# Three real products instead of four in half of a forward transform, and an edge column computed inside the loop before it

## The chip, the cores and the metric

The kernel runs on one core of a Trainium2 chip. TensorE multiplies matrices into PSUM, VectorE and ScalarE read PSUM and SBUF, GpSimd does small elementwise work in SBUF, and DMA queues that are fed by SyncE, ScalarE and GpSimd move data. The metric is the time of one execution on the device in microseconds, and lower is better. The kernel before takes 1229.07 us (median of 3 runs, 1228.78 to 1231.65).

## The reference

The input x has 2048 rows (s) of 1024 values. Its rows are normalised, and two branches work on the result.

```python
xn = _layernorm(x, axis=-1)
X = rfft2(xn) * (w_r + 1j * w_i)          # branch A: filter in the frequency domain
s = irfft2(X)
h = silu(einsum("bsd,df->bsf", xn, w1))   # branch B: 1024 -> 3584 -> 1024
g = silu(einsum("bsf,fd->bsd", h, w2))
return x + s * g
```

Both branches must come out in single precision. TensorE works on halves, so a factor is split into a high and a low half (float16), and a product is the sum of high x high, high x low and low x high: three passes.

## The kernel before

TensorE's order is one list that Python writes at build time. Its backbone is branch B: 112 blocks of 24 matmuls of 512 columns (`mm1`, tile `pa`, L458), then 56 blocks of 42 such matmuls (`mm2`, tile `pb`, L541 to L543). The 56 blocks are seven products (a fast 2x2 scheme over halves of the matrices) of eight blocks each; `pb2_0` is product 2, block 0. Their left factors `ht` are fetched from HBM on ScalarE's queue two blocks ahead (`load_h`, L517).

Branch A is a background job in five stages, each a Python generator that issues a little work at each `yield`: layer norm, forward transform over the row (`fd_gen`), forward transform over s and filter (`f_gen`), the edge column (`edge_gen`), inverse transforms (`i_gen`). `work()` is called after each block, and inside each `mm2` block after 21 of its 42 matmuls; each call advances the background by up to three steps, and stops earlier when a metered VectorE clock is more than `LEAD` = 1 us ahead of a metered TensorE clock. The meter charges VectorE 0.12 us and 1.05 ns per element of a row for each instruction. So the places of the background's matmuls among the blocks are fixed at build time; at run time each engine goes through its own list, and semaphores make it wait.

The forward transform over s: s is written as 4a + c, and `fd_gen` leaves, for each c and each column block j of 128 frequencies, complex values V split in halves, stored in HBM as `vd[j]`. `f_gen` has 16 units u = 4q + j. A unit takes frequency class q, computes for each c the complex product of a 128x128 matrix (`kq`) with V (`mat`, tile `fx`), combines the four c by a radix-4 step (`xb`, `xd`, `X`), multiplies by the filter (`wq`, `T1`, `T2`, `Y`), makes the first radix-4 step of the inverse (`yb`, `yd`, `Z`; GpSimd does an eighth of it), and splits the result in halves (`zq`; ScalarE writes the high one in `high_z`, L992, VectorE the low one in `low_z`, L997). `mat` is:

```python
for c in range(4):
    o = ps[:, c].rearrange("m r k -> m (r k)")
    for n, (kh, vh) in enumerate(((0, 0), (0, 1), (1, 0))):
        nc.tensor.matmul(o, k[:, c, kh, 1], v[:, c, vh], ...)                              # L965, 256 columns
        nc.tensor.matmul(ps[:, c, 0], k[:, c, kh, 2], v[:, c, vh, 128:256], ...)           # L966, 128
        nc.tensor.matmul(ps[:, c, 1], k[:, c, kh, 0], v[:, c, vh, 0:128], ...)             # L967, 128
```

A unit's result is one tile of two PSUM banks, and the pool `pt` has two of them. ScalarE copies the half c = 2, 3 to SBUF (`xc`, L986), and VectorE adds and subtracts PSUM and copy (L1015, L1016). `mat(u + 1)` is issued inside unit u. `zq` holds four units in one buffer: the first unit of a class (u = 4, 8, 12) can only write it when the four DMAs `zd<-zq` of the class before have landed, and that wait stands in ScalarE's list, in front of whatever ScalarE has to do next.

The edge column (frequency 512 of the row transform, and its partner 0) needs every class, so `edge_gen` ran as a job of its own after unit 15: 12 small copies on GpSimd, nine float32 matmuls of 8 and 24 columns (`eps`, L1096 to L1098; each goes through TensorE in two passes), some 32 GpSimd instructions, and a store and four loads through HBM (`zpd`, `zps`). Then the job `switch` closes the filter's buffers and opens those of the inverse: `zt` is loaded from `zd` (L1173), GpSimd writes the edge column into it (`edge_in`, L1184), and the first inverse matmuls (`iu`, L1215) read it.

## Time and profile before

| what | value |
|---|---|
| time, median of 3 runs | 1229.07 us (1228.78 to 1231.65) |
| time of the profiled execution | 1231.15 us |
| its span, first to last instruction | 1229.4 us |
| TensorE busy | 1218.5 us, 6992 matmuls |
| VectorE busy | 999.7 us, 81% |
| ScalarE busy | 471.5 us, 38% |
| forward transform over s (`fx`) | from 570.7 to 814.5 us |
| `eps` | from 838.0 to 840.8 us |
| first `iu` | at 892.3 us |

A profile's matmul lasts longer than the step to the next one, because matmuls are pipelined. Where several follow each other, the price of one is the distance between two starts. The span leaves out 1.75 us of the profiled execution's time. A row of the timeline reads: start, duration, engine, line, operation, out<-in, shape, count, and in brackets how long the engine had been idle and what it waited for.

### The profile page before, as it was taken

How to read it: one execution, taken by the hardware profiler on the slowest of the kernel's cores; microseconds unless marked ns; L12 is line 12 of the kernel's file. 1: busy time of each engine (PE TensorE's matmuls, PEld its weight loads, DVE VectorE, ACT ScalarE, POOL GpSimd, SP SyncE). 2: the span in 40 equal slices, each digit the busy share in tenths (PEclk: the TensorE clock that was granted, in tenths of full speed). 3: DMA queues.
4: the chain of work that ended last, by engine and by line, in shares of the span. 5: the costliest groups of instructions: out<-in, count | busy, mean ns of one | idle time of the engine just before them, and what ended most of it. 6: DMA issues, size and time to landing. Idle time of an engine off the chain costs nothing.

```text
span 1229.4 us, 19034 instructions
## 1 busy us (share of the span) xinstructions
PE 1218.5 (99%) x6992; PEld 619.8 (50%) x6992; DVE 999.7 (81%) x1974; ACT 471.5 (38%) x614; POOL 119.7 (10%) x247
## 2 busy tenths in 40 slices
PE   8999999999999999999999999999999999999998
PEld 5544445444544454445445555544455545555545
DVE  7778998799899889887969899885186678798885
ACT  6675343343554555435433222122032222233212
POOL 3320000000000000010001121114111111000000
PEclk9999999999999999999999999999999999999999
DMA  8887477645669797759899989987979999998686
GB/s 250 186 199 182 139 235 218 202 131 166 201 188 299 226 296 225 217 188 285 178 301 236 299 249 192 276 243 244 285 195 286 276 291 331 305 355 327 199 268 253
DMA packets 279550, 295.77 MB, mean 241 GB/s; under 512 B 48544, under 2 KB 207264, under 8 KB 279072
## 3 DMA queue, kind: packets, MB, share of 16 engines
q1 hardware_dynamic: 259440, 235.76, 65.6%
q10 hardware_dynamic: 15984, 51.45, 12.2%
q0 software_dynamic: 4032, 7.34, 3.5%
q8 instruction: 55, 0.90, 0.3%
q14 instruction: 39, 0.32, 0.1%
HBM read 185.95 MB, written 102.25 MB: 234 GB/s over the span
## 4 chain that ended last, share of the span: by engine, by line
PE 70%; DVE 11%; DMA 8%; issue 3%; ACT 3%; POOL 0%; SPq 0%; ACTq 0%; DVEq 0%; POOLq 0%
PE pa L458 41%; PE pb L541 8%; PE pb L543 8%; PE pb L542 8%; DVE Z L1066 2%; DMA zd<-zq 2%; PE id L1305 2%; DVE T L1031 1%; ACT xp L740 1%; DMA sd<-s 1%; DVE w L256 1%; PE iu L1215 1%; DMA ht<-hd_sum_d 1%; DMA wq<-in_A_w_i_dram 1%; DVE zq L997 1%
## 5 line engine op out<-in xcount | busy, mean ns | idle before, releaser
L458 PE MATMUL pa<-xnT,w 128*128 128x512 f16 x2688 | 584.1, 379 | 1.2 <-ACT w L253 0.7
L458 PEld LDWEIGHTS <-w 128*128 128x128 f16 x2688 | 261.4, 98 | 313.1 <-issue 1.2
L541 PE MATMUL pb<-w,ht 128*128 128x512 f16 (+2 forms) x812 | 301.2, 373 | 0.0
L543 PE MATMUL pb<-w,ht 128*128 128x512 f16 (+2 forms) x812 | 301.0, 373 | 0.0
L542 PE MATMUL pb<-w,ht 128*128 128x512 f16 (+2 forms) x812 | 301.0, 372 | 0.0
L543 PEld LDWEIGHTS <-ht 128*128 128x128 f16 x812 | 79.6, 98 | 91.5 <-issue 0.8
L542 PEld LDWEIGHTS <-ht 128*128 128x128 f16 x812 | 79.6, 98 | 87.1 <-issue 0.8
L541 PEld LDWEIGHTS <-ht 128*128 128x128 f16 x812 | 79.6, 98 | 87.0 <-issue 0.6
L467 ACT ACTIVATE h<-pa,s 128x512 f32<-128x512 f32 x112 | 75.8, 678 | 117.6 <-PE pa L458 94.1
L253 ACT ACTIVATE w<-jr,sc 128x512 f16<-128x512 f32 x98 | 68.1, 713 | 84.4 <-DMA jr<-in_B_w_dram 35.9
L253 ACT ACTIVATE hosum<-hr,hs 128x1536 f16<-128x1536 f32 x28 | 44.1, 1574 | 78.3 <-DVE hr L497 41.4
L256 DVE SCALAR_TENSOR_TENSOR w<-jr,sc,w 128x512 f16<-128x512 f32 x98 | 71.1, 744 | 2.7 <-ACT w L253 2.7
L253 ACT ACTIVATE hoone<-h,hs 128x2048 f16<-128x2048 f32 x28 | 56.0, 1999 | 44.6 <-issue 26.5
L256 DVE SCALAR_TENSOR_TENSOR hoone<-h,hs,hoone 128x2048 f16<-128x2048 f32 x28 | 65.6, 2344 | 7.1 <-ACT hoone L253 7.1
L992 ACT ACTIVATE zq<-Z,zs 128x1024 f16<-128x1024 f32 x16 | 18.4, 1148 | 99.1 <-DVE Z L1066 50.9
L256 DVE SCALAR_TENSOR_TENSOR hosum<-hr,hs,hosum 128x1536 f16<-128x1536 f32 x28 | 50.8, 1813 | 2.5 <-ACT hosum L253 2.5
L496 DVE TENSOR_TENSOR hr<-h 128x1024 f32<-128x1024 f32 x28 | 34.2, 1222 | 22.8 <-ACT h L467 22.8
L634 ACT ACTIVATE pl<-pl,c 128x512 f32<-128x512 f32 (+2 forms) x28 | 17.4, 656 | 67.9 <-DVE pl L610 39.1
L965 PE MATMUL fx<-vq,kq 128*128 128x256 f16 x192 | 43.2, 273 | 0.0
L253 ACT ACTIVATE w<-w1r,rs 128x1024 f16<-128x1024 f32 x28 | 31.9, 1144 | 29.0 <-DVE w L256 19.1
L966 PE MATMUL fx<-vq,kq 128*128 128x128 f16 x192 | 42.0, 219 | 0.0
L967 PE MATMUL fx<-vq,kq 128*128 128x128 f16 x192 | 42.0, 219 | 0.0
(225 smaller groups left out, 1514.0 us busy)
## 6 DMA issues: line engine op xcount, KB each, us to landing
w1r<-in_B_w_dram SPq DMA_DIRECT2D x28, 512.0 KB, 6.5
hd_sum<-hosum SPq DMA_DIRECT2D x56, 256.0 KB, 2.9
hd_one<-hoone SPq DMA_DIRECT2D x56, 256.0 KB, 3.7
hd_dif<-hoone SPq DMA_DIRECT2D x56, 256.0 KB, 3.2
w2m<-in_B_w_dram SPq DMA_DIRECT2D x28, 512.0 KB, 6.2
ht<-hd_dif ACTq DMA_DIRECT2D x32, 448.0 KB, 6.2
jr<-in_B_w_dram SPq DMA_DIRECT2D x56, 256.0 KB, 6.9
ht<-hd_sum ACTq DMA_DIRECT2D x32, 448.0 KB, 5.9
```

The source lines that it names most:

```text
L253: nc.scalar.activation(hi, raw, AF.Copy, scale=scale)
L256: nc.vector.scalar_tensor_tensor(lo, raw, scale, hi, op0=OP.mult, op1=OP.subtract)
L458: nc.tensor.matmul(ps, w[:, wh, d], xt[:, xh, d], start=(n == 0), stop=(n == 23))
L467: nc.scalar.activation(hq[:, 2 * (c % 2) + f % 2], ps, AF.Silu, scale=s1[:, f:f + 1])
L496: tt(sums[:, 0:2], hq[:, 0::2], hq[:, 1::2], op=OP.subtract)
L541: nc.tensor.matmul(ps, hh[:, 0], w[:, 0], start=first, stop=False)
L542: nc.tensor.matmul(ps, hh[:, 0], w[:, 1], start=False, stop=False)
L543: nc.tensor.matmul(ps, hh[:, 1], w[:, 0], start=False, stop=last)
L965: nc.tensor.matmul(o, k[:, c, kh, 1], v[:, c, vh], start=(n == 0), stop=False)
L966: nc.tensor.matmul(ps[:, c, 0], k[:, c, kh, 2], v[:, c, vh, 128:256], start=False, stop=False)
L967: nc.tensor.matmul(ps[:, c, 1], k[:, c, kh, 0], v[:, c, vh, 0:128], start=False, stop=(n == 2))
L1066: eng.tensor_tensor(Z[:, ns, pos], x0[:, :, ls], x1[:, :, ls], op=o_)
```

## The change

For the classes q = 2 and 3 (units 8 to 15, `THREE`) a complex product is made of three real ones. With k = a + ib and V = x + iy, the products are cos (x + y), (sin - cos) y and (-sin - cos) x, and the real and the imaginary part are the first plus one of the other two. The constants for these classes change accordingly (the same array, the same size). `fd_gen` computes x + y for them, splits it in halves and stores it in HBM (`vs`). `mat` issues 36 matmuls of 128 columns in place of 12 of 256 and 24 of 128. A unit now needs three planes for each c, so it takes two PSUM tiles, one for c = 0, 2 and one for c = 1, 3. ScalarE copies the common plane of both tiles to SBUF, twice side by side (`xo`), and VectorE adds the other two planes to it; `xb` and `xd` then read SBUF alone. The meter is set back by 0.8 us for the two new VectorE instructions in each step of `fd_gen`.

The edge column's generator is started in unit 12 and advanced from inside units 12 to 15; its small loads of filter columns (`xsv`) are issued two per unit in units 0 to 7 instead of one per unit in all 16. Its scratch and its permutation matrix live in the pool of `mm2`'s tiles, and its PSUM tile comes from the pool of the blocks (`ff`). `fs` and `fx` tiles of the output stage get a pool of their own, opened with the inverse.

```diff
+    k[list(THREE)] = np.stack([np.cos(th), np.sin(th) - np.cos(th), -np.sin(th) - np.cos(th)], 3)[list(THREE)]
...
         def high_r(j):
+            both[j] = ap.tile([128, len(THREE), 2, 128], F16, name=f"vt{c}_{j}", tag="wd", bufs=3)
+            nc.scalar.activation(both[j][:, :, 0], total[j], AF.Copy, scale=2.0**-21)
...
         def low_r(j):
...
+            nc.vector.scalar_tensor_tensor(both[j][:, :, 1], total[j], 2.0**-21, both[j][:, :, 0], op0=OP.mult, op1=OP.subtract)
...
+            defer(2, lambda: nc.sync.dma_start(vs[j][:, :, c], both[j]))
...
+            total[j] = ap.tile([128, len(THREE), 128], F32, name=f"vt{c}_{j}", tag="E", bufs=1)
+            some = o[j][:, THREE[0]:THREE[-1] + 1]
+            nc.vector.tensor_tensor(total[j], some[:, :, 0:128], some[:, :, 128:256], op=OP.add)
+            clock["dve"] -= 0.8
...
+        def load_s(u):
+            q, j = u // 4, u % 4
+            if u < 16 and q in THREE:
+                B["s"][u] = bp.tile([128, 4, 2, 128], F16, name=f"vs{u}", tag="xc", bufs=2)
+                nc.sync.dma_start(B["s"][u], vs[j][:, q - THREE[0]])
...
         def mat(u):
             q = u // 4
+            v, k = B["v"].pop(u), B["k"][q]
+            if q in THREE:
+                t_ = B["s"].pop(u)
+                for half in range(2):
+                    ps = pt.tile([128, 2, 512], F32, name=f"fx{u}_{half}", tag="ft")
+                    for i, c in enumerate((half, half + 2)):
+                        for g, src in enumerate((t_[:, c], v[:, c, :, 128:256], v[:, c, :, 0:128])):
+                            for n, (kh, vh) in enumerate(((0, 0), (0, 1), (1, 0))):
+                                nc.tensor.matmul(ps[:, i, 128 * g:128 * g + 128], k[:, c, kh, g], src[:, vh], start=(n == 0), stop=(n == 2))
+                    psx[u, half] = ps
+                return
...
         def copy(u):
-            cps[u] = bp.tile([128, 2, 256], F32, name=f"xc{u}", tag="xc", bufs=1)
+            if u // 4 in THREE:
+                cps[u] = bp.tile([128, 2, 2, 2, 128], F32, name=f"xo{u}", tag="T1", bufs=1)
+                for half in range(2):
+                    nc.scalar.activation(cps[u][:, half], psx[u, half][:, :, 0:128].unsqueeze(2).broadcast_to([128, 2, 2, 128]), AF.Copy)
+                return
+            cps[u] = bp.tile([128, 2, 256], F32, name=f"xc{u}", tag="xc", bufs=2)
...
+            if q in THREE:
+                for half in range(2):
+                    planes = psx.pop((u, half))[:, :, 128:384].rearrange("m i (r k) -> m i r k", r=2)
+                    tt(cpy[:, half], cpy[:, half], planes, op=OP.add)
...
+            load_s(u + 2)
...
+            if u == 12:
+                B["edge"] = edge_gen()
+            if u > 14:
+                next(B["edge"])
...
+            if u == 12:
+                next(B["edge"])
+            if u > 13:
+                next(B["edge"])
...
+            if u > 12:
+                next(B["edge"], None)
             yield 2.9
         high_z(15)
+        next(B["edge"], None)
...
-        ps = pt.tile([128, 1024], F32, name="eps", tag="ft")
+        ps = pf.tile([128, 512], F32, name="eps", tag="ff")
...
-                add(bg, edge_gen())
```

What this moves is not in these lines. On TensorE, the nine `eps` matmuls stood between `pb2_2` and `pb2_3`, behind all units:

```order
L543 MATMUL pb2_2_8243<-w2_2_1_7436,ht2_2_1_8046 128x512
L1096 MATMUL eps_8328<-edge_8315,perm_8042 128x24
L1097 MATMUL eps_8328<-edge_8315,perm_8042 128x8
L1098 MATMUL eps_8328<-edge_8315,perm_8042 128x8
...
L541 MATMUL pb2_3_8343<-w2_2_0_7088,ht2_3_0_8171 128x512
```

and now stand two blocks earlier, between `pb2_0` and `pb2_1`, ahead of the last unit's matmuls:

```order
L547 MATMUL pb2_0_8186<-w2_2_1_7559,ht2_0_1_7917 128x512
L1153 MATMUL eps_8261<-edge_7912,perm_7913 128x24
...
L545 MATMUL pb2_1_8275<-w2_2_0_7208,ht2_1_0_8051 128x512
...
L547 MATMUL pb2_1_8275<-w2_2_0_7208,ht2_1_0_8051 128x512
L986 LDWEIGHTS kq3_7204
L986 MATMUL fx15_0_8303<-vs15_8040,kq3_7204 128x128
```

Unit 15's matmuls stood in the middle of `pb2_0` before and stand in the middle of `pb2_1` now, one block later. From `pb2_2` on, the two lists are the same but for line numbers, and `iu1_0` stands in the middle of `pb3_0` in both.

On ScalarE, at the first unit of the last class, the write of `zq3` that waits for the DMAs of `zq2` stood in front of the loads for block `pb2_0`:

```order
L253 ACTIVATE w2_2_1_7436<-jr41_7568,sc2_231 128x512
L986 ACTIVATE xc13_7821<-fx13_7778 128x512
L992 ACTIVATE zq3_7838<-Z12_7825,zs_220 128x64x16
L517 DMA ht2_0_0_7849<-hd_dif_0_0_88 128x1792
L517 DMA ht2_0_1_7851<-hd_dif_0_0_88 128x1792
```

Now those loads come first, and it stands in front of the loads for the next block:

```order
L521 DMA ht2_0_0_7915<-hd_dif_0_0_92 128x1792
L521 DMA ht2_0_1_7917<-hd_dif_0_0_92 128x1792
L1016 ACTIVATE xo13_7993<-fx13_0_7949 128x512
L1016 ACTIVATE xo13_7993<-fx13_1_7968 128x512
L1025 ACTIVATE zq3_8036<-Z12_7998,zs_224 128x64x16
L521 DMA ht2_1_0_8051<-hd_dif_0_0_92 128x1792
L521 DMA ht2_1_1_8053<-hd_dif_0_0_92 128x1792
```

On SyncE, the stores of the last class (`zd<-zq3`) stood well ahead of the loads that read them (`zt1`):

```order
L412 DMA jr51_8267<-in_B_w2_dram 128x512
L1001 DMA zd0_79<-zq3_7838 128x2x1024
L1001 DMA zd1_80<-zq3_7838 128x2x1024
...
L412 DMA jr54_8424<-in_B_w2_dram 128x512
L1152 DMA zpd_83<-zp_216 128x64
L412 DMA jr55_8459<-in_B_w2_dram 128x512
L1150 DMA zps_217<-zpd_83 64x4x8 x4
L412 DMA jr56_8488<-in_B_w2_dram 128x512
L1173 DMA zt1_8497<-zd1_80 64x8x512 x4
```

Now they come behind the edge column's store, three loads of w2 (`jr`) later:

```order
L416 DMA jr54_8569<-in_B_w2_dram 128x512
L1209 DMA zpd_87<-zp_220 128x64
L1034 DMA zd0_83<-zq3_8036 128x2x1024
L1034 DMA zd1_84<-zq3_8036 128x2x1024
...
L416 DMA jr55_8607<-in_B_w2_dram 128x512
L1207 DMA zps_221<-zpd_87 64x4x8 x4
L416 DMA jr56_8636<-in_B_w2_dram 128x512
L1231 DMA zt1_8645<-zd1_84 64x8x512 x4
```

The stores are nearer to the loads that read them.

44 lines of the change are left out of this document (28 added, 16 removed).

## The prediction

> **What bounds the kernel now.** I read the page first, then who TensorE waits for, then the timeline where the change acts.
>
> ```profile
> PE 1218.5 (99%) x6992; PEld 619.8 (50%) x6992; DVE 999.7 (81%) x1974; ACT 471.5 (38%) x614; POOL 119.7 (10%) x247
> PE 70%; DVE 11%; DMA 8%; issue 3%; ACT 3%; POOL 0%; SPq 0%; ACTq 0%; DVEq 0%; POOLq 0%
> PE eps L1096 <- POOL edge L1089: 0.7, 1, 0.7
> PE eps L1098 <- POOL edge L1092: 0.2, 1, 0.2
> ```
>
> TensorE is busy 99% of the span, and behind its first microseconds its waits are under 1 us each. So time is won where TensorE gets less to do or waits less, and other engines count only if they make it wait. The two lines of `eps` are among those few waits.
>
> **The three products.** The last unit's matmuls before, and the first inverse matmuls, in TensorE's timeline:
>
> ```profile
> 811.85 0.27 PE L965 MATMUL fx<-vq,kq 128*128 128x256 f16 x1
> 811.96 0.22 PE L966 MATMUL fx<-vq,kq 128*128 128x128 f16 x1
> 812.01 0.22 PE L967 MATMUL fx<-vq,kq 128*128 128x128 f16 x1
> 812.07 0.27 PE L965 MATMUL fx<-vq,kq 128*128 128x256 f16 x1
> ...
> 814.50 0.38 PE L541 MATMUL pb<-w,ht 128*128 128x512 f16 x1
> 892.34 2.84 PE L1215 MATMUL iu<-kk,zt 128*128 128x128 f16 x48
> 895.02 0.38 PE L541 MATMUL pb<-w,ht 128*128 128x512 f16 x1
> L1215 PEld LDWEIGHTS <-zt x192: 97/98/98, 892.1 to 986.1; 128*128 128x128 f16 x192
> ```
>
> A unit takes 811.85 to 814.50, 2.65 us. In its place come 36 matmuls of 128 columns, each with its own weight load. The `iu` rows are such a stream: 48 in 895.02 - 892.34 = 2.68 us, 55.8 ns each. So a new unit costs 36 x 55.8 = 2.01 us, and eight units save 8 x 0.64 = **5.1 us** of a queue that hardly ever waits.
>
> **The edge step on TensorE.**
>
> ```profile
> 836.95 0.38 PE L543 MATMUL pb<-w,ht 128*128 128x512 f16 x1
> 838.01 0.40 PE L1096 MATMUL eps<-edge,perm 128*128 128x24 f32 x2 [0.68 <-POOL edge L1089]
> ...
> 840.13 0.38 PE L1096 MATMUL eps<-edge,perm 128*128 128x24 f32 x2
> 840.35 0.37 PE L1097 MATMUL eps<-edge,perm 128*128 128x8 f32 x2
> 840.57 0.37 PE L1098 MATMUL eps<-edge,perm 128*128 128x8 f32 x2
> 840.80 0.38 PE L541 MATMUL pb<-w,ht 128*128 128x512 f16 x1
> 841.01 0.38 PE L542 MATMUL pb<-w,ht 128*128 128x512 f16 x1
> 841.23 0.57 PE L543 MATMUL pb<-w,ht 128*128 128x512 f16 x1
> ...
> 844.85 0.38 PE L543 MATMUL pb<-w,ht 128*128 128x512 f16 x1
> 837.58 0.37 POOL L1089 COPY edge<-xsv 128x24 f32<-128x24 f32 x1
> 840.16 0.18 POOL L1092 COPY edge<-xsv 128x6 f32<-128x6 f32 x1
> 840.00:845.00 5.00, 5.00 (x20) 2.40 (x21) 3.87 (x5) 3.10 (x5) 3.51 (x11) 0.66 0.58 173
> ```
>
> A 512-column step is 0.216 us, so TensorE was free at 837.17 and back on blocks at 840.80: 3.63 us, paced by GpSimd's copies (837.58 to 840.34). The last three, with nothing to wait for, take 0.67 us, so nine need 2.0 us, and at best 1.6 us are won. At worst the wait only moves: the copies now follow unit 13's `Z` on GpSimd, which follows `zq3` through VectorE, the stage where VectorE is latest (below). Nothing in the rows says on which side it falls, and I take the middle, **0.8 us**.
>
> Behind it nine matmuls take 841.23 to 844.85, 3.62 instead of 9 x 0.216 = 1.94 us: the granted clock of 0.66 over these 5 us is 3.4 us at half speed, **1.7 us** lost. With the thin stretch down from 3.6 to some 2.8 us I take this as gone; if it stays, the term is 0. [...]
>
> The runs fit this: the profiled execution took 1231.15 us, 2.08 more than the median of the runs, which is little more than one such slow stretch. I sum against 1231.15; the median may not have had the stretch at all.
>
> **What is priced at nothing, and its cover.** VectorE and ScalarE get more work.
>
> ```profile
> 100.00:560.00 460.00, 459.52 (x2353) 217.04 (x2352) 403.53 (x821) 214.60 (x251) 19.88 (x38) 1.00 0.69 209
> 700.00:812.00 112.00, 112.00 (x711) 61.34 (x710) 100.99 (x186) 23.16 (x32) 18.52 (x34) 1.00 0.94 240
> L240 DVE TENSOR_TENSOR Ro<-Rb 128x256 f32<-128x256 f32 x16 | 6.8, 424 | 0.4
> L1015 DVE TENSOR_TENSOR xb<-fx,xc 128x512 f32<-128x512 f32 x9 | 6.1, 679 | 0.0
> L986 ACT ACTIVATE xc<-fx x16: 577/597/598, 573.6 to 814.8; 128x512 f32<-128x512 f32 x16
> L997 DVE SCALAR_TENSOR_TENSOR zq<-Z,zs,zq 128x1024 f16<-128x1024 f32 x11 | 14.0, 1276 | 10.5 <-ACT zq L992 10.5
> ```
>
> In `fd_gen`, 16 x 2 VectorE instructions on 256 elements, at 0.42 us (the L240 row), are 13.6 us; VectorE's columns of the first row leave it 56 us idle there. In the units, 8 x 2 additions of 512 elements, at 0.68 us (L1015), are 10.9 us; VectorE idles 11.0 us from 700 to 812, but 10.5 us of such idling (the L997 row, over 700 to 850) is waiting for `zq`. So the units have no free VectorE time, and the stage gets longer; the meter sees this and puts unit 15 one block later (9.06 us, the order above), so that TensorE has blocks to do. ScalarE: 16 copies of 256 elements and eight more of 512, each under the 0.60 us of L986, 14.4 us at most, of over 330 idle in both rows together. DMA: 16 stores and eight loads of 256 KB, 2% of 296 MB; the eight loads fall where DMA is at 0.94, 2.1 MB or 8.7 us of it at 240 GB/s. Without cover each of these would cost its full sum; as long as the blocks stand in between, I take **0**.
>
> **Two places with little room.**
>
> ```profile
> 789.55 3.61 SPq L1001 DMA_DIRECT2D zd<-zq  x4
> 802.08 1.15 ACT L992 ACTIVATE zq<-Z,zs 128x1024 f16<-128x1024 f32 x1 [14.69 <-DMA zd<-zq]
> 802.10 0.82 ACTq L517 DMA_DIRECT2D ht<-hd_dif  x2
> 842.36 3.40 SPq L1001 DMA_DIRECT2D zd<-zq  x4
> 858.69 4.75 SPq L1173 DMA_DIRECT2D zt<-zd  x4
> 884.04 1.75 POOL L416 DMA_DIRECT2D jr<-in_B_w_dram  x2 [18.35 <-DMA jr<-in_B_w_dram]
> 885.21 0.85 POOL L1184 COPY zt<-zps 128x16 f16<-128x16 f16 x1
> ```
>
> First, ScalarE stood 14.7 us in front of `zq3`, and the loads of `pb2_0` went out only at 802.10. That block starts 21 x 0.216 before 811.85, at 807.3: its factors had 5.2 us. The new order puts these loads ahead of the wait, and behind it those of `pb2_1`, which starts one block and `eps` later. Nothing lost.
>
> Second, `iu1_0` at 892.34 reads `zt` after GpSimd's copy (885.21 to 886.06), and that copy stands behind two `jr` additions which waited for loads queued after `zt`: 6.3 us of room. The stores `zd<-zq3` were issued 16.3 us ahead of `zt`. Block `pb2_3` starts at 840.80, and 42 x 0.216 and the 1.7 us of slow clock later, at 851.55, `pb2_4`; `zt` went out 7.1 us into that, `iu1_0` starts 40.8 us into it in both lists. The stores were issued 1.6 us into `pb2_3`; now they come one block later, 1.6 us into `pb2_4`. From first issue to last landing they took 802.08 - 789.55 = 12.5 us in the rows above, under load; so `zt` goes out at 14.1 at the latest and at 7.1, as before, at the earliest: 0 to 7.0 us later, against 6.3 of room. I take **0**; with the worst landing 0.7 us is lost, and 4 if SyncE or the DMAs are another 3.3 late.
>
> Sum: 1231.15 - 5.1 - 0.8 - 1.7 = **1223.5 us**. About 0.3%, 3.7 us, is what a measurement of this kernel can tell from no change; the bounds around the median are 1225.4 and 1232.8.
>
> **Rivals.**
>
> *A new wait takes part of it.* At `iu1_0`, or at an `fx` whose two PSUM tiles VectorE has not read yet: both tiles now belong to one unit, so `mat(u + 1)` needs all of unit u's sums, one block (9.06 us) after they were issued. For it: up to all of the 6.3 us can be used, VectorE stood still 8.5 us at `zq3`. Against: blocks in between. A wait of 2 to 4 us gives 1225.5 to 1227.5. Chance 0.25.
>
> *VectorE becomes the bound of the units.* If the `zq` wait keeps its 10.5 us, the 10.9 us find no idle time and the block of room is spent elsewhere, TensorE waits for all of it at `fx9` to `fx15`: 1223.5 + 10.9 = 1234.4, slower. It decides from 9 us of lateness on, and the list was stretched by a block against just that. Chance 0.06.
>
> *The matmuls don't get shorter.* If weight loads paced the stream at the 98 ns of their rows, a unit would take 36 x 0.098 = 3.5 us, 0.9 more than before: 1231.15 + 8 x 0.9 - 2.5 = 1235.9. The `iu` row, with the same loads at 55.8 ns, speaks against it. Chance 0.02. [...]
>
> *Everything falls well.* No wait at `eps` at all: 1231.15 - 5.1 - 1.6 - 1.7 = 1222.7, or less where VectorE's list gains. Chance 0.12.
>
> **How the numbers follow.** The forecast has 0.55, with a range of its own of 1222 to 1225.4. Faster by over 0.3%: 0.55 + 0.12 + a third of the first rival, 0.75. Slower: 0.07. Within: 0.18. The range runs from 1221, a little below the best case, to 1227.5, the far end of the first rival.
>
> **What would show it.** 36 `fx` matmuls in 2.0 us for units 8 to 15, and 2.65 for 0 to 7. The stretch from the end of `pb2_0` to the start of `pb2_1` of 2.0 to 3.6 us, and whether the granted clock drops behind it. No wait of TensorE for VectorE at `fx9` to `fx15`. `iu1_0` without a wait for `zt`; a gap before it is the first rival. If TensorE's sum falls by 5 us and the span does not, I have missed a wait; if the units take 2.65 us still, the first term is wrong.

## The result: slower by 1.6%, and the profile after

The changed kernel takes 1252.03 us (median of 6 runs, 1249.13 to 1254.65), the kernel before 1232.14 us (6 runs, 1228.78 to 1237.21; the three of the section before are among them): the ratio is 1.0164, with a 95% interval of 1.0136 to 1.0192. The forecast was 1223.5 us. The profiled execution took 1251.9 us, with a span of 1250.0, 20.6 us more than before. Two runs of the fourth group of experiments below took over twice as long as the rest of their kernels' runs (2609.66 us in e15, its profiled one, and 2852.46 us in the kernel before), so the ratios, though not the medians, leave them out, and the trace of e15 is not read.

TensorE's busy time on the page of the changed kernel, and below it the list of what TensorE waited for:

```profile
PE 1222.6 (98%) x6992; PEld 619.8 (50%) x6992; DVE 1021.5 (82%) x2022; ACT 478.0 (38%) x638; POOL 120.2 (10%) x247
```

```profile
PE pa L462 <- ACT h L471: 5.7, 2, 4.3
PE fx L986 <- ACT zq L1025: 4.6, 1, 4.6
PE eps L1153 <- POOL edge L1146: 2.9, 1, 2.9
PE pa L462 <- DVE w L260: 2.1, 1, 2.1
PE iu L1281 <- DVE ub L1290: 2.0, 1, 2.0
```

Before, no wait behind the first microseconds was over 1 us. Now there are 17.3 us of them, at four places, and TensorE's "busy" time has gone up although it has less to do. The windows around these places say why (the columns behind POOL are the granted clock, the DMA share and GB/s):

```profile
540.00:550.00 10.00, 6.48 (x18) 2.24 (x17) 9.35 (x15) 7.32 (x9) 0.70 (x1) 0.66 0.27 93
564.00:574.00 10.00, 7.16 (x26) 2.95 (x26) 5.96 (x5) 5.94 (x7) 0.00 (x0) 0.83 0.86 302
720.00:732.00 12.00, 7.44 (x52) 4.61 (x50) 11.93 (x23) 1.63 (x2) 1.84 (x4) 0.72 0.72 219
834.00:846.00 12.00, 10.60 (x48) 6.14 (x49) 11.90 (x23) 3.94 (x7) 3.59 (x15) 0.72 0.97 228
```

A clock of 0.66 over 10 us is 6.8 us at half speed. It begins within the waits, at 543.2 us: in the timeline TensorE works again from 544.70 to 550, 5.3 us of the 6.8, and half of that, 2.7 us, is lost on top of two waits of 1.5 and 2.1 us. In the second window, 0.83, it is 3.4 us after a wait of 4.3, so 1.7 us more. So the first stall cost 1.8 times its length and the second 1.4 times, and the two windows together come to 12.1 us.

TensorE's list can be counted through block by block in both traces. The lag of a block (its start after minus before), taken where both lists have the same units behind them, tells where the 20.6 us came in:

| up to the start of | before | after | lag | what came in |
|---|---|---|---|---|
| `pb0_0` | 630.48 | 643.82 | 13.3 | 0.8 at the start of the kernel; 12.5 in the last forward steps over the row, 540 to 571 us |
| `pb1_0` | 718.90 | 738.58 | 19.7 | 7.0 in unit 8, less 0.64 that its matmuls save |
| `pb2_0` | 807.31 | 823.16 | 15.9 | units 9 to 14 save 6 x 0.64 = 3.8 |
| `pb2_4` | 851.55 | 870.18 | 18.6 | the edge step costs 3.4 more, unit 15 saves 0.64 |
| second group of `iu0` | 1058.91 | 1079.56 | 20.6 | 2.0, a wait for VectorE in the inverse transform |

The forecast's first term is in there as it stood: in the timeline a unit of three products takes 743.12 to 745.13, 2.01 us instead of 2.65, and eight of them save 5.1 us. The rest of the table is waits and the slow clock behind them, but for the 0.8 at the start. There ScalarE delivers `x` 0.65 us later than before, and the granted clock is halved for 3.4 us from 10.7 us on; other traces have such a stretch (e2, e3, e8) or not (e1, e5, e11), so it does not belong to the change.

```profile
743.12 0.33 PE L986 MATMUL fx<-vs,kq 128*128 128x128 f16 x3
...
745.13 0.38 PE L545 MATMUL pb<-w,ht 128*128 128x512 f16 x1
```

**The first place, 540 to 571 us.** From the timeline of ScalarE's and SyncE's work:

```profile
533.60 0.87 SPq L885 DMA_DIRECT2D vs<-vt  x1
537.55 0.42 ACT L877 ACTIVATE vt<-vt 128x256 f16<-128x256 f32 x1 [13.03 <-DMA vs<-vt]
...
565.67 0.39 ACTq L952 DMA_DIRECT2D kq<-in_kc_dram  x1
566.11 0.69 ACT L471 ACTIVATE h<-pa,s 128x512 f32<-128x512 f32 x1 [10.74 <-DMA vs<-vt]
```

ScalarE stood still for 13.0 us in front of the high half of a sum, until the store of an earlier sum had landed, and 10.7 us in front of the first load of `kq`, which it issues itself and which waits for the forward pool to be given back, so for the last store of a sum. Both times the evacuations `h` of TensorE's blocks were queued behind it, and the first time a high half `w` as well, whose low half TensorE waited for next (2.1 us).

**The second place, unit 8.** TensorE stopped in the middle of a unit, between its two PSUM tiles:

```profile
721.19 0.50 PE L986 MATMUL fx<-vq,kq 128*128 128x128 f16 x6
726.25 0.50 PE L986 MATMUL fx<-vs,kq 128*128 128x128 f16 x3 [4.56 <-ACT zq L1025]
...
725.51 0.68 DVE L1057 TENSOR_TENSOR xd<-fx,xc 128x512 f32<-128x512 f32 x1
```

The second tile is the one that unit 7 used, and VectorE read it until 726.19 (`xd`). The list names ScalarE's `zq` instead, which ended 0.04 us later and does not touch this tile. Before, `fx8` took the tile of unit 6, which VectorE had left 11.8 us earlier (at 699.95; `fx8` starts at 711.71).

**The third place, the edge step.**

```profile
834.07 0.86 POOL L1116 TENSOR_TENSOR Z<-yd 128x32 f32<-128x32 f32 x2
834.88 0.38 POOL L1146 COPY edge<-xsv 128x24 f32<-128x24 f32 x1
...
835.31 0.40 PE L1153 MATMUL eps<-edge,perm 128*128 128x24 f32 x2 [2.92 <-POOL edge L1146]
...
838.48 0.59 PE L545 MATMUL pb<-w,ht 128*128 128x512 f16 x1
```

GpSimd's copies stand behind its share of unit 13's `Z`, which VectorE delivers late. TensorE was free at 832.23 and back on blocks at 838.48: 6.25 us instead of 3.63, and 6.8 us at half clock instead of 3.4.

### The profile page after: what moved, and what is told of

Its sections match the earlier page's. It is cut to its first block, busy times and chain, and to the rows that moved or that the text cites. A ratio compares the mean times of both kernels' runs of the same rounds, so it can differ in the third digit from the quotient of the medians.

```text
span 1250.0 us, 19127 instructions
## 1 busy us (share of the span) xinstructions
PE 1222.6 (98%) x6992; PEld 619.8 (50%) x6992; DVE 1021.5 (82%) x2022; ACT 478.0 (38%) x638; POOL 120.2 (10%) x247
## 4 chain that ended last, share of the span: by engine, by line
PE 61%; DVE 14%; DMA 12%; ACT 3%; issue 3%; SPq 2%; ACTq 0%; POOL 0%; DVEq 0%
PE pa L462 36%; PE pb L546 7%; PE pb L545 7%; PE pb L547 7%; DMA zd<-zq 3%; DVE Z L1116 2%; PE id L1363 2%; DMA vs<-vs 2%; DMA kk<-in_kc_dram 1%; DVE w L260 1%; ACT xp L744 1%; DVE T L1078 1%; DVE zq L1030 1%; PE iu L1273 1%; DMA out_dram<-pl 1%
## 5 line engine op out<-in xcount | busy, mean ns | idle before, releaser
L257 ACT ACTIVATE hoone<-h,hs 128x2048 f16<-128x2048 f32 x28 | 55.9, 1997 | 46.9 <-DVE h L505 18.6
L420 POOL DMA_DIRECT2D jr<-in_B_w_dram x28 | 24.7, 977 | 169.3 <-DMA jr<-in_B_w_dram 78.0
L291 POOL TENSOR_SCALAR s<-e 128x2 f32<-128x2 f32 (+1 forms) x15 | 3.4, 228 | 362.7 <-DVE e L288 362.7
L282 DVE TENSOR_REDUCE m1b<-w1r 128x1 bf16<-128x1024 f32 x22 | 26.8, 1216 | 14.0 <-DMA w1r<-in_B_w_dram 14.0
```

Source lines behind the costliest of these rows:

```text
L257: nc.scalar.activation(hi, raw, AF.Copy, scale=scale)
L282: nc.vector.tensor_reduce((m1 if i < 6 else m1b)[:, i:i + 1], raw[i], axis=AX.XY, op=OP.max, apply_absolute_value=True)
L420: nc.gpsimd.dma_start(raw[n], w2_block(*todo[n], 1), accum_op=OP.add)
```

## The experiments

Eighteen kernels ran, in five groups; a group shares its runs of the kernel before. The ratio is to the kernel before of the same group.

| run | what | median us | before | ratio (95%) |
|---|---|---|---|---|
| e1 | as changed, two sums share a buffer | 1248.98 | 1230.08 | 1.0148 (1.0114 to 1.0182) |
| e2 | as changed, without the sums | 1237.81 | 1230.08 | 1.0062 (1.0036 to 1.0088) |
| e3 | as changed, edge column as before | 1259.41 | 1230.08 | 1.0226 (1.0192 to 1.0260) |
| e4 | edge column's move alone | 1240.31 | 1230.08 | 1.0073 (1.0046 to 1.0100) |
| e5 | e1, `kq` loaded by SyncE | 1252.49 | 1229.87 | 1.0171 (1.0134 to 1.0208) |
| e6 | e5, meter set back by 0.7 | 1248.99 | 1229.87 | 1.0150 (1.0104 to 1.0196) |
| e7 | e6, edge copies earlier | 1251.37 | 1229.87 | 1.0170 (1.0129 to 1.0211) |
| e8 | e7, `zd` stored by GpSimd | 1251.78 | 1229.87 | 1.0164 (1.0123 to 1.0205) |
| e9 | e2, edge copies earlier, no additions | 1235.71 | 1230.32 | 1.0027 (1.0005 to 1.0049) |
| e10 | e4, edge copies earlier | 1235.90 | 1230.32 | 1.0044 (1.0026 to 1.0062) |
| e11 | the sums alone | 1242.40 | 1230.32 | 1.0090 (1.0067 to 1.0113) |
| e12 | e5, one more pause before unit 0 | 1245.23 | 1230.32 | 1.0106 (1.0079 to 1.0134) |
| e13 | the 36 matmuls alone | 1230.78 | 1232.28 | 0.9985 (0.9966 to 1.0003) |
| e14 | e13 and the loads | 1232.70 | 1232.28 | 1.0001 (0.9980 to 1.0021) |
| e15 | e13, copies and additions through T1 | 1235.35 | 1232.28 | 1.0018 (0.9998 to 1.0039) |
| e16 | e15 with a buffer of its own | 1233.24 | 1232.28 | 1.0009 (0.9991 to 1.0027) |
| e17 | e13, `pl` loaded by GpSimd | 1233.34 | 1231.77 | 1.0008 (0.9989 to 1.0026) |
| e18 | e13 without the loads of x | 1223.08 | 1231.77 | 0.9927 (0.9900 to 0.9954) |

Runs of one kernel spread by 4 to 12 us (e18: 1.1), so terms of 1 or 2 us are read from the traces, not from the medians. A trace is of one execution: those of e9 and e10 are of the fastest of their runs, 5.3 and 3.4 us under the median.

### First group: what each part costs

**e1, two sums share a buffer.**

```diff
-            both[j] = ap.tile([128, len(THREE), 2, 128], F16, name=f"vt{c}_{j}", tag="wd", bufs=3)
+            if j % 2 == 0:
+                o["vt"] = ap.tile([128, 2, len(THREE), 2, 128], F16, name=f"vp{c}_{j}", tag="wd", bufs=3)
+            both[j] = o["vt"][:, j % 2]
```

> Edit: the sums of two neighbouring j share one buffer of the pool's tag, so a sum never takes the buffer of the sum just before it; everything else is as in the changed kernel. Theory A (shared buffer): ScalarE's 13.0 us wait for the store of the sums ahead of 537 us goes, the matmuls' waits at 540 and 562 us shrink, and with them the two stretches at half clock behind them: 1252 - 8 to 12.5, that is 1240 to 1244 us. Theory B (the forward additions themselves, 13.6 us more on VectorE, 16 more stores on the sync queue, make the forward transform late wherever the sums lie): 1250 to 1252 us, and the waits stay.

The median fell by 3 us only. The 13.0 us wait is gone, and with it the stall at 540 us. But the second stall grew, from 4.3 to 6.0 us, and unit 8 still waits. ScalarE's timeline at the second stall:

```profile
559.99 0.39 ACTq L954 DMA_DIRECT2D kq<-in_kc_dram  x1
560.42 0.69 ACT L471 ACTIVATE h<-pa,s 128x512 f32<-128x512 f32 x1 [10.72 <-DMA vs<-vp]
```

The lag at `pb0_0` is 8.4 us instead of 13.3. So the shared buffer was one of two causes in this stretch. A new wait of 3.2 us, ahead of the first inverse transform, takes part of the gain.

**e2, without the sums.**

```diff
-            both[j] = ap.tile(...)           # the sums: formed, split, stored
...
-            clock["dve"] -= 0.8
...
-                nc.sync.dma_start(B["s"][u], vs[j][:, q - THREE[0]])
+                nc.sync.dma_start(B["s"][u], vd[j][:, q, :, :, 0:128])
```

> Leaves out the forming, splitting and storing of the sums over the two planes and the credit on the planner's VectorE clock; the units of classes 2 and 3 read the first plane where the sum should stand, so three products per complex one and the edge column are as in the changed kernel and the forward transform is as before. Theory A: no wait at 540 to 566 us (12.5 us less than the changed kernel); unit 8 stands one block later in TensorE's order, as in the kernel before, so the wait of fx8_1 (4.6 us, and 3.4 us of half clock) goes too: 1252 - 20 = 1231 to 1233 us, of which the units' matmuls are -5.1 us and the edge matmuls about +4. Theory C (a unit of three products waits because it needs both accumulators, wherever it stands): the wait at the first unit of three products stays, 1237 to 1241 us.

No wait in the forward transform and none at unit 8, as theory A had it: a unit that needs both tiles does not stall by itself. But 1237.8 is 5 us above its sum. In the trace TensorE is 4.0 us ahead of the kernel before at `pb2_1`, and then loses 7.2 at the edge step (a wait of 3.6, and 10.2 us at half clock) and 4.5 in the inverse (a wait of 3.5 for `ub`, and 3.4 us at half clock).

Why are VectorE and GpSimd late there, with no sums? `zq` shows it (e2's timeline):

```profile
734.15 3.41 SPq L1025 DMA_DIRECT2D zd<-zq  x4
...
747.80 1.15 ACT L1016 ACTIVATE zq<-Z,zs 128x1024 f16<-128x1024 f32 x1 [5.21 <-DMA zd<-zq]
```

VectorE had finished this `zq` at 728.72; before, at 725.04, and there the stores went out at 725.06. Here they stood 5.4 us in SyncE's queue behind two loads of weights (`jr`) that went out between 727.33 and 733.08. So the next `zq` started at 747.80 instead of 737.84, and VectorE, which follows it, was 10 us later. VectorE's waits for `zq` from 570 to 860 us were 13.2 us with all its additions, and 15.6 before.

**e3, edge column as before.** The edge column's pieces of the diff are undone.

> Three products and the sums as in the changed kernel; the edge column as in the kernel before (a step of its own behind the last unit). Theory A: everything of the changed kernel but the edge matmuls' longer step and the second 3.4 us of half clock, 4.3 us together: 1247 to 1249 us. Theory D (the edge column's place within the units delays the units and VectorE beyond its own step, the 2 us wait ahead of the inverse included): 1244 us or less.

The opposite came out: 7 us more. The edge step still waits 2.7 us for GpSimd, now after unit 15, and the inverse waits 4.2 us for `ub`. The edge column's late place was not the fault of its move; VectorE is late in either place.

**e4, the edge column's move alone.**

> The edge column within the last units, as in the changed kernel; four products per complex one in all units, no sums. By my prediction's own term: 0.8 to 2.5 us faster than before, 1229 to 1231 us. Theory A: the edge matmuls wait for GpSimd's copies, which stand behind the last butterfly of unit 13, 4.3 us more than before: 1235 to 1237 us.

As theory A had it or worse: with four products, no sums and no additions, the move alone costs 10 us. The list of waits and GpSimd's timeline:

```profile
PE eps L1142 <- POOL edge L1135: 5.4, 1, 5.4
```

```profile
812.05 1.02 POOL L1105 TENSOR_TENSOR Z<-yb 128x32 f32<-128x32 f32 x2 [18.12 <-DVE yb L1084]
813.04 0.85 POOL L1105 TENSOR_TENSOR Z<-yd 128x32 f32<-128x32 f32 x2
813.83 0.37 POOL L1135 COPY edge<-xsv 128x24 f32<-128x24 f32 x1
```

GpSimd was idle for 18 us before `Z`; the copies, which need nothing from unit 13, stood behind it in its list.

### Second group: mending the stalls one by one

Each kernel here contains the one before it.

**e5, `kq` by SyncE.**

```diff
-            nc.scalar.dma_start(t_, kf[q])
+            nc.sync.dma_start(t_, kf[q])
```

> The first experiment (two sums to a buffer), and the load of the filter's constants kq is issued by the sync engine in place of ScalarE; the rest as in the changed kernel. Theory E (ScalarE stands still for 10.7 us, because it issues the first kq load, which waits until the forward pool's last store, that of the sums, has landed; the evacuations of the matmuls' results are queued behind it): the 6.4 us wait of the matmuls at 555 us and its 6.8 us at half clock go, 9.8 us less than the first experiment: about 1239 us. Theory B (VectorE itself is late with the forward transform): the wait stays, with VectorE as the one waited for: 1246 us or more.

Theory E is right on the place of the wait and wrong on the time. The wait for `h` is gone, but the median did not fall. The list of waits:

```profile
PE fx L988 <- ACT zq L1027: 6.0, 1, 6.0
PE fx L995 <- DMA vq<-vd: 4.6, 1, 4.6
```

TensorE now runs on to unit 0, whose operand `vq` is loaded behind the same release, and waits there; and unit 8 waits longer. Smaller waits are new as well: 2.4 us for factors `ht`, 3.3 at the edge step, 2.1 ahead of the first inverse transform.

**e6, the meter set back by 0.7.** `clock["dve"] -= 0.7` in place of 0.8.

> As the run with kq on the sync engine, and the credit on the planner's VectorE clock is 0.7 in place of 0.8, which puts the units 0 to 8 back to the blocks of TensorE's order where they stood before (unit 8 behind pb0_7 in place of pb0_6). Theory F (at unit 8 TensorE waits because the unit, now in need of both accumulators, stands one block earlier): the 4.3 us wait inside fx8 and its 6.8 us at half clock go, 7.7 us less: about 1231.5 us. Theory C (the need of both accumulators alone, with VectorE late): a wait of over 2 us stays at fx8; 1236 to 1239 us.

At unit 8 the wait fell from 6.0 to 1.6 us without a slow stretch, so theory F holds there: with 0.8 us given back for each step, a little more than the 0.78 us that the meter had charged, units 0 to 8 had moved up by one block. But the number changes the forward transform's order too, and there ScalarE waits again (5.0 us for `h` at 557 us), unit 11 waits 2.0 us for VectorE's additions (`xo`) of the unit before, and the edge step waits 4.0 us. The median fell by 3.5 us, not 21.

**e7, the edge copies earlier.**

```diff
-            if u > 13:
+            if u > 12:
                 next(B["edge"])
             yield 2.3
...
-            if u > 12:
+            if u > 13:
                 next(B["edge"], None)
```

> As the run before, and GpSimd's twelve copies for the edge column are issued ahead of unit 13's butterfly, not behind it. Theory G (the edge matmuls wait because GpSimd's list puts the copies behind its share of that butterfly, which waits for VectorE): the wait of 3 to 4 us ahead of the edge matmuls goes, and the stretch at half clock shrinks from 6.8 or 10.2 us to 3.4: 5 to 7 us less than the run before, about 1225 us. Theory H (VectorE is late by more than that everywhere from unit 8 on): the loss turns up at the inverse transform instead; 1229 us or more.

Both theories in one run: the edge step's wait is gone (G), and the time did not fall (H), because the inverse transform now waits 7.6 us for the edge column's rows, with 10.2 us at half clock:

```profile
PE iu L1275 <- POOL zt L1244: 7.6, 1, 7.6
```

**e8, `zd` stored by GpSimd.** `nc.gpsimd.dma_start(zd[c][:, q], ...)` at once, in place of the deferred SyncE store.

> As the run before, and the stores zd<-zq are issued by GpSimd at once, not by the sync engine one step later, behind loads that wait. Theory I (VectorE's 10 to 15 us of waiting for zq within the units are no room: each is a round trip of zq through the store zd, whose start moves with VectorE's work and is held up in the sync queue): VectorE's wait for zq falls below 8 us, the last unit ends 5 to 10 us earlier than in the run before, and a wait for ub at the inverse transform, if there is one, goes: 0 to 5 us less. Theory J (room enough; the store's place does not matter): no difference over 1 us.

Theory I fails in this form. The stores went out right behind VectorE (745.86 us, VectorE done at 745.32), yet the last landed at about 763 us, and VectorE waited 18.2 us for `zq`. With the hold-up in SyncE's queue gone, the way from issue to landing got longer: 8.4 to 15.0 us for each of the four, against 6.4 to 10.1 in e7.

### Third group: parts alone, again

**e9, without the sums and without the additions.**

```diff
-                    planes = psx.pop((u, half))[:, :, 128:384].rearrange("m i (r k) -> m i r k", r=2)
-                    tt(cpy[:, half], cpy[:, half], planes, op=OP.add)
+                    psx.pop((u, half))
```

> As the second experiment (no sums formed; 1237.8 us), and it also leaves out VectorE's two additions of the three products in each of the units 8 to 15 (1.27 us a unit, 10.2 us in all; the butterfly reads ScalarE's copies alone), with GpSimd's copies for the edge column ahead of unit 13's butterfly. Theory K (VectorE is the path of the units: the 10.2 us of additions come on top of its waits for zq, they do not go into them): unit 15 is done some 10 us earlier than in the second experiment, no wait of the matmuls over 1 us from 640 us on, and the 5.1 us of shorter matmuls are kept: 1224 to 1228 us. Theory L (the two accumulators, ScalarE's doubled copies and the order of the sync queue delay the units): 1233 to 1238 us.

Theory K fails: 10.2 us of VectorE's work were taken away, and the last `Z` was done at 852.9 us instead of 856.0 in e2; the first write of `zq2` started at 748.2 us, and at 747.8 in e2. The time went into longer waits (18.0 us for `zq` in front of VectorE, 13.2 in e2). So between `zq`s the round trip through HBM sets the pace, not the additions. TensorE waited too, 4.9 us at 770 us. The list names VectorE's `xb`, but the factors `ht` that this block reads were loaded from 759.51 on and took 15.4 us to land, at 774.9, just before TensorE went on.

**e10, the edge move with the copies earlier.** The diff of e7 on e4.

> As the fourth experiment (edge column within the last units, four products; 1240.3 us), with GpSimd's copies ahead of unit 13's butterfly. Theory G: the 5.4 us wait ahead of the edge matmuls and the 10.2 us at half clock behind it go: 1228 to 1231 us, level with the kernel before or up to 2.5 us under it, as my prediction had it. Theory H: the matmuls now reach the inverse transform before the edge column's rows are loaded, and wait there: 1234 us or more.

The wait and the slow stretch at the edge step are gone, and TensorE is 3.6 us ahead of the kernel before at `pb2_4`: all that my two edge terms promised (2.5 us), and more. Then it loses 5 us in the inverse, where `zt` now comes too late, as theory H had it:

```profile
PE iu L1262 <- POOL zt L1231: 2.9, 1, 2.9
PE iu L1270 <- DVE ub L1279: 2.0, 1, 2.0
```

**e11, the sums alone.** The `fd_gen` part of the diff on the kernel before.

> The kernel before, with the sums formed, split and stored in the forward transform as the changed kernel does, and not read by anyone; four products in all units, edge column as before. Theory A: the waits at 540 to 566 us and the half clock behind them: 10 to 13 us more than before, 1240 to 1244 us; no wait at unit 8, which needs one accumulator. My prediction (the additions lie in VectorE's idle time): 1230 to 1232 us.

This is theory A: `pa` waits 5.3 us for `h` and 2.1 for `w`, the lag at `pb0_0` is 12.55 us, unit 8 does not wait, and the median is 12.1 us up. This is the largest single cost of the change, and my prediction had it at 0.

**e12, one more pause.** A second `yield PAUSE` behind `load_k(0)` in e5.

> As the run with two sums to a buffer and kq on the sync engine (1252.5 us), with one more pause in the planner's list ahead of unit 0, which puts the units 0 to 8 back to the blocks where they stood before and leaves the forward transform's order alone. Theory M (in that run the sums were ready in time for TensorE, but unit 0 stood one block too early for the load of vq, and unit 8 one block too early for VectorE): the waits at 565 us (4.6 us) and in unit 8 (6.0 us) go with their half clock, 8.0 and 9.4 us: 1235 to 1238 us. Theory B (VectorE is late with the forward transform wherever the units stand): the waits stay or move, 1245 us or more.

The lag at `pb0_0` is 2.7 us; it was 13.3 in the changed kernel, 8.4 in e1 and 6.9 in e5. So of the forward transform's 12.5 us, some 10 were buffer, queue and place. The rest of the forecast was too good: waits of 2.3 us for `vq`, of 3.4 at unit 8 and at the edge step and of 4.4 in the inverse remain, and the median is 1245 us.

### Fourth and fifth group: why the units lose more than they save

**e13, the matmuls alone.** `mat` as in the change, on the kernel before:

```diff
+            if q in THREE:
+                t_ = v[:, :, :, 0:128]
+                for half in range(2):
...
+                                nc.tensor.matmul(ps[:, i, 128 * g:128 * g + 128], k[:, c, kh, g], src[:, vh], ...)
```

> The kernel before with the 36 matmuls of three products in units 8 to 15 on two accumulators each, and nothing else: no sums, no loads of them (the first plane is multiplied in their place), the copies and butterflies read the two other products' columns with the sizes of before, the edge column as before. By the matmul term of my prediction (5.1 us less): 1225 to 1227 us, with the edge step's wait as before. If two accumulators a unit make TensorE wait: 1229 us or more, with a wait at an fx.

> As e13, and each of the units 8 to 15 loads 256 KB more through the sync queue (bytes of the stored forward transform in place of the sums), which its first product reads. If the loads are covered: as e13 within 1 us. If they hold the stores of zq back in the queue and the transfers, and with them VectorE: 3 to 8 us more than e13, with longer waits for zq.

> As e13, and ScalarE's two copies per unit of the first product into the buffer T1 and VectorE's two additions as in the changed kernel (no loads). My prediction (additions and copies are covered): as e13 within 1 us. Theory P (ScalarE's copy waits until VectorE has freed T1, and the weights' halves, the loads behind them and the stores of zq are queued behind it; the additions come on top): 5 to 10 us more than e13, 1231 to 1236 us.

> As e15, with a buffer of their own for ScalarE's copies in place of T1. If the shared T1 is the cause: within 2 us of e13. If the additions are: within 2 us of e15.

e13 is the surprise: nothing but shorter matmuls, and the median gains 1.5 us where 5 were expected, with an interval that reaches over no change. In its trace TensorE is 8.0 us ahead of the kernel before from `pb2_5` on (the 5.1 us, and the edge step without its wait and its slow stretch), up to the block at 1050 us. There (list of waits, then TensorE's and VectorE's timeline):

```profile
PE iu L1242 <- DVE ub L1251: 6.6, 1, 6.6
```

```profile
1053.17 0.69 DVE L600 TENSOR_TENSOR pl<-pl,pb 128x512 f32<-128x512 f32 x1 [3.63 <-DMA pl<-pd]
...
1057.29 2.78 PE L1242 MATMUL iu<-kk,zt 128*128 128x129 f16 x24 [6.62 <-DVE ub L1251]
1059.86 0.63 PE L543 MATMUL pb<-w,ht 128*128 128x512 f16 x1
...
1063.02 0.38 PE L545 MATMUL pb<-w,ht 128*128 128x512 f16 x1
```

VectorE waits for the load `pl<-pd` that it needs ahead of `ub`, TensorE waits for VectorE 6.6 us, and then runs at half clock for 5.5 us (its 512-column steps, the rows of 0.63 us, are 0.43 us apart instead of 0.216, to 1062.8). All 8 us are gone. Before, VectorE waited as long for the same load, and TensorE, 8 us later, hardly noticed:

```profile
1056.35 0.69 DVE L598 TENSOR_TENSOR pl<-pl,pb 128x512 f32<-128x512 f32 x1 [3.67 <-DMA pl<-pd]
1058.91 1.55 PE L1223 MATMUL iu<-kk,zt 128*128 128x129 f16 x24 [0.23 <-DVE ub L1232]
```

So in e13 the load came 3.2 us earlier than before, and TensorE 8 us earlier.

The loads (e14) and the copies and additions (e15, e16) move the medians by 2 to 5 us more, less than the spread allows to rank; in e14 and e16 the same wait for `ub` is there (5.6 and 4.5 us). The buffer T1 does hold ScalarE up: in the changed kernel it waits 7.0 us in front of unit 8's copy for VectorE's `yd`, the last to read T1, and the copy starts 5.7 us after the unit's last matmul (728.03); in e16, with its own buffer, unit 8's copy starts right behind the first half of the matmuls:

```profile
733.74 0.60 ACT L1016 ACTIVATE xo<-fx 128x512 f32<-128x512 f32 x1 [7.03 <-DVE yd L1096]
```

```profile
713.21 0.60 ACT L1001 ACTIVATE xo<-fx 128x512 f32<-128x512 f32 x1
```

The last `Z` of e16 is done at 847.1 us, 9 us earlier than in e2. (e16 has no extra loads and no move of the edge column, so the two differ in more than the buffer. e14 and e16 also give the output stage a pool of its own, as the change does.)

**e17 and e18, what holds VectorE up at 1050 us.** `nc.gpsimd.dma_start(t_, pd[k, j])` in place of SyncE's; and, for e18:

```diff
+            if (name, tag) == ("fx", "fx"):
+                t_.append(t_[0])
+                continue
```

> As e13 (matmuls of three products alone), with the loads pl<-pd issued by GpSimd, out of the sync queue. If their place in that queue is what holds VectorE up at 1050 us: the wait for ub falls from 6.6 to under 3 us and its half clock goes: 5 to 8 us less than e13, 1223 to 1226 us. If the transfers are at their limit: within 2 us of e13.

> As e13, without the 256 KB loads of x into the buffer fx for the final sums (about 24 loads, 6 MB; the other operand is added twice in their place). If the transfers are at their limit and hold VectorE up at 1050 us: the wait for ub falls to under 2 us and the gain is kept: 1220 to 1225 us. If it is the order of the queue alone: the wait stays over 4 us, 1227 us or more.

The place in SyncE's queue is not it: with `pl` out of that queue the wait is 6.3 us. Without the loads of x (19 loads, 5.0 MB by the pages) there is no wait of TensorE behind the first microseconds, the 8 us stay (the lag is -7.9 to -8.3 us from `pb2_5` to the inverse's last transform), and the time is 1223.08 us. The windows of the kernel before, of e13 and of e18 (the last two columns are the DMA share and GB/s):

```profile
940.00:1000.00 60.00, 60.00 (x384) 31.76 (x383) 48.87 (x134) 15.53 (x29) 9.00 (x11) 1.00 0.98 296
1000.00:1060.00 60.00, 59.77 (x394) 32.18 (x393) 42.98 (x93) 14.30 (x31) 4.85 (x6) 1.00 0.97 311
```

```profile
940.00:1000.00 60.00, 60.00 (x384) 31.75 (x383) 51.74 (x140) 16.96 (x30) 7.20 (x9) 1.00 0.99 291
1000.00:1060.00 60.00, 53.38 (x363) 30.24 (x362) 40.73 (x94) 11.63 (x27) 4.60 (x6) 0.97 0.96 322
```

```profile
940.00:1000.00 60.00, 60.00 (x385) 31.67 (x383) 51.73 (x140) 16.97 (x30) 7.18 (x9) 1.00 0.98 289
1000.00:1060.00 60.00, 60.00 (x401) 32.64 (x399) 46.64 (x106) 14.55 (x32) 4.92 (x6) 1.00 1.00 344
```

From 940 to 1060 us the DMA engines are busy 97 to 98% of the time in the kernel before already. But this share is no ceiling that explains the loss: e18 loses nothing at 0.98 and 1.00, and moves more in these 120 us than the others (316 GB/s; 306 in e13, 304 before). The issue of the load says more (e13, then e18, then e17):

```profile
1049.02 2.46 SPq L536 DMA_DIRECT2D pl<-pd  x2
```

```profile
1039.61 3.33 SPq L536 DMA_DIRECT2D pl<-pd  x2
```

```profile
1048.04 0.55 POOL L536 DMA_DIRECT2D pl<-pd  x1 [10.74 <-DMA pd<-pl]
```

In e13 the load takes 4.1 us, no longer than before (4.6); it goes out late. It waits for a buffer, on whichever queue it stands, until an earlier store `pd<-pl` has landed: in e13 that store was issued at 1040.61 and took 8.3 us (6.9 before, 9.5 in e17), in e18 it was issued at 1034.02 and took 5.5 us. So this is a ring through HBM, of load, addition, store and buffer, and TensorE's lead did not shorten it: 8.0 us of lead in e13, and the addition behind the load started 3.2 us earlier than before. With fewer loads beside it, in e18, it turned faster: the load went out at 1039.61 us, not 1049.02. Whether more buffers would do the same was not tested. e18 is no version of the kernel, since it leaves out work, and a kernel before without these loads was not run.

No version was found that beats the kernel before. The best case of the idea, e13, has yet to pay for loads, copies, additions and sums, and gains some 4 us at most (1232.28 x 0.0034, the far end of its interval).

## Why the prediction was wrong, by its own steps

**The matmul term (-5.1 us): right in size, wrong as a gain.** 2.01 us a unit, as worked out; the rival of weight loads that pace the stream is out. But the step "five microseconds of a queue that hardly ever waits" took the 99% for proof that TensorE is the only bound. e13 and e18 show a second one right behind it: at 1050 us VectorE, and with it TensorE, waits for the ring of loads and stores of `pl`, and the time that TensorE wins ahead is waited out there. In the kernel before VectorE already waited 3.67 us for that load, with TensorE arriving just behind it; I looked at the waits of TensorE only.

**The forward additions (0): the step that failed most, 12.5 us.** I set 13.6 us of VectorE's work against 56 us of its idle time and 14.4 of ScalarE's against over 330, averages over 460 us. Neither sum was the question. ScalarE works off its list in order, and the new high half waits for a buffer whose store must have landed, in a tag of three that a second job uses too (e1), and, at the end of the transform, ScalarE's own load of `kq` waits for the last of the new stores (e5). The diff shows both: the tag "wd", and stores added in front of a pool's release. In the kernel before ScalarE already stood 6 us in front of that load, with no wait of TensorE (its timeline before):

```profile
553.02 0.39 ACTq L940 DMA_DIRECT2D kq<-in_kc_dram  x1
553.46 0.69 ACT L467 ACTIVATE h<-pa,s 128x512 f32<-128x512 f32 x1 [6.01 <-DMA vd<-Rs]
```

In the changed kernel it stood 10.7 us there, and these 4.7 us more made TensorE wait 4.3: the cover was all but used up. I listed the 16 stores by their bytes (as 256 KB each; they are 128) and not by who waits for their landing.

**The edge step (-0.8) and its slow stretch (-1.7): wrong in sign, +3.4 together.** The prediction named the reason ("the copies now follow unit 13's `Z` on GpSimd") and then took a middle between "moves" and "gone". e4 and e7 show the price and that the order on GpSimd alone is the cause of the wait at that place; with the copies moved, the two terms came out at 3.4 us (e10; 0.2 of its 3.6 us were there from the start), and the inverse took them back. That a thin stretch of 2.8 us leaves the clock whole, as the 1.7 us assumed, was my estimate, and no run shows it: in the changed kernel and the experiments the edge step either waited 2.7 us or more or did not wait, and in e10, with no wait and no slow stretch, it took 1.92 us (807.15 to 809.07).

**The first rival (a wait of 2 to 4 us at an `fx` or at `iu1_0`, 0.25): right in place, short in price.** The `fx` wait was 4.6 us, and TensorE worked 4.7 us at half clock behind it (726.25 to 730.92), so 2.3 more: 6.9 of the 7.0 in the table. Two things were missed. The meter's credit was a little too large, and moved units 0 to 8 up by one block (e6, e12): I had followed unit 15 through the new order, not unit 8. And VectorE came to unit 8 late from the stretch before: in e12, with the units back in their places, 3.4 us of wait remain, and in e2, without the sums, none.

**VectorE as the bound (0.06): wrong in its mechanism.** With 10.9 us more for VectorE to do, the `zq` waits shrank by 2.4 us only (15.6 before, 13.2 in e2), and with the additions gone again they grew (e9). Nor did TensorE wait for it at every unit from `fx9` on, as this rival had it; single waits are in some experiments (2.0 us at unit 11 in e6). I had treated this idle time as a wait to be kept or filled. It is a round trip whose start moves with VectorE's own work and with SyncE's queue (5.4 us of it in e2).

**The two places with little room: no wait in the changed kernel, but no proof either.** Neither `pb2_0`'s factors nor `iu1_0` made TensorE wait, with TensorE 19 us later. In other kernels with the edge move `iu1_0` did wait: 2.9 us in e10 (at `pb2_4` 3.6 us ahead of the kernel before), 7.6 in e7 (6.7 behind it), 3.2 in e1 (12.1 behind) and 2.1 in e5 (20.1 behind). In e7 and e10 it waited for the copy behind the `jr` additions that the prediction describes. So the 0 came out for the changed kernel partly by luck.

What stays open: how the 2 to 5 us of e14 to e16 divide among loads, copies and additions, what the ring of `pl` needs to turn faster, and whether a layout with both PSUM tiles free and the sums elsewhere would keep e13's gain.

## What to carry to other kernels

A new instruction is covered only if every wait that it brings into its engine's list is covered: ask for each new tile whose store or reader must be done before its buffer comes round again, and what is queued behind the one that waits (here `h` and `w`, behind ScalarE's waits of 13.0 and 10.7 us). Idle time averaged over a stage said nothing about that here: VectorE's 56 us stood against 13.6 us of new work, and 12.5 us were lost. And an engine at 99% was not the only bound: before counting time saved on it as gain, look further down the span for a place where another engine waits for data and the busy one arrives just behind it, because there the time can be waited out again, as all 8 us were in e13. The waits of that other engine showed the place (3.67 us in the kernel before); the DMA share alone did not (0.97 there, and 1.00 in e18, which kept its gain).

## What was not expected of the hardware

A wait of TensorE can cost more than its length, 1.4 and 1.8 times in the first two windows above. Over all traces, the last microseconds of the kernel apart, the stretches at half clock lasted 3.41, 6.83 or 10.2 us, one, two or three times one length. Some begin within the wait (in the changed kernel at 543.2 and 724.1 us, in waits that ended at 544.70 and 726.25), and half of what TensorE works in them is lost: its 512-column steps took 0.43 us in them (e13), not 0.216. Away from the edge step and the kernel's start, no single wait under 2.0 us was followed by one (two of 1.5 and 2.1 us that stood 0.6 us apart were, at 541 to 545 us). Waits of 2.0 to 2.9 us were at times (2.02 us in e6 and 2.44 in e5 yes; 2.94 in e10 no), longer ones always. At the thin edge step a wait of 0.7 us was enough in the kernel before, and the longest stretch followed 3.6 us there (e2) as well as 7.6 us in the inverse (e7).

And the spread of a kernel's runs came with its transfers: the runs of e18 lie between 1222.80 and 1223.87 us, 1.1 us, those of e13, with 5 MB more to load, between 1225.68 and 1233.73. That the transfers cause the spread was not tested.
